# The last 64 rows of a Q projection in two row tiles, two heads at once, beside the paired remainder scores

## The chip, the cores and the metric

The kernel runs on one core of a Trainium2 chip. The metric is device time in microseconds of that core; lower is better. Engines are called PE (TensorE, the matrix unit), DVE (VectorE), ACT (ScalarE), POOL (GpSimd) and SP (SyncE, which here only issues DMAs). PE reads weights and a moving operand from SBUF and writes PSUM, which has eight banks; DVE and ACT read PSUM and write SBUF.

## The reference

Two independent problems A and B of the same shape are computed and their outputs are put side by side. Each is grouped-query attention against a cache of keys and values:

```python
B, Sq, D = 16, 80, 576
Hq, Hkv, Sk, Dh = 32, 16, 512, 128          # two query heads share one K/V head
q = (x @ wq)                                # [B*Sq, 576] @ [576, 4096]
scores = einsum("bhqd,bhkd->bhqk", q, k) * Dh ** -0.5
p = softmax(scores, axis=-1)
o = einsum("bhqk,bhkd->bhqd", p, v)
out = o @ wo                                # [B*Sq, 4096] @ [4096, 576]
result = concatenate([out_A, out_B], axis=-1)
```

All inputs are bfloat16. The contraction of the Q projection has 576 rows, which is four times 128 and a rest of 64.

## The kernel before, in words

**Units.** The work of both problems is cut into 128 units; a unit is one batch with four K/V heads, that is eight query heads of 80 rows. Eight units with the same heads form an octet (variable `goct`, 16 of them), which is what the Q projection works by. For each unit PE computes scores in five tiles: the 160 query rows of one K/V head are 128 + 32, so each of the four heads gives one main tile (line 658, 128 rows by 512 keys), and the four rests of 32 rows are put into one remainder tile by four matmuls that stand side by side in column tiles of 32 (line 644, `tile_position=(0, 32 * g4)`). The remainder tiles of two units are issued together as a group (`em_qkr`, lines 640 to 655; `GRP` and `GR` give the group sizes 1, 1, 2, 2, ...).

**A tile's way.** DVE takes the row maximum (line 667), ACT the exponential with the row sum (671), DVE the reciprocal (677), POOL the normalisation (680), PE four transposes (686), DVE the copy back to SBUF (692, 694), and PE multiplies with V (731). ACT evicts that result (747), and PE's output projection (781) reads it. For 45 units the transposes of the remainder tile are made by a DMA instead (698).

**The Q projection** (line 540, `em_qp`). x is held transposed in `xT`, five chunks of 128 rows; since 576 is 4.5 chunks, the fifth chunk takes x's last 128 columns (line 463, and 485 for problem B), of which the first 64 have already been used, and the weights that meet them are zeros (`wqz`, line 395: rows 0 to 63 of the fifth chunk of `wq_sb`). For each octet and each of its eight heads there are two pieces, one of six batches (480 columns) and one of two (160 columns); each piece is five matmuls into one PSUM bank, and one eviction with the scale, by ACT (551) or DVE (552), whichever the planner finds free. In the first octet the narrow piece comes first.

**Order.** Every operation is put into a list with a due time (`key`), what it reads and writes, and an assumed duration; the planner (`_Sched.arrange`, lines 135 to 253) runs through the list with these durations, takes at each engine the most urgent operation that is ready, and gives out PSUM banks from the list of the operation's class (`BANKS`: S scores, T transposes, O attention output, M, M0, M1, ML projections). The result is a fixed order for each engine, with semaphore waits between them. Each engine runs its own list in that order. A bank is given out again when its last reader is done. `ahead` moves an operation forward in the choice without moving its due time.

**DMAs.** All loads but the first two of `wq` are issued by SP, in one list: K by a transposing DMA (612) into five buffers, V (616) into four, `wq` in an "a" part (514, 512 rows) and a "b" part (517, the last 64 rows), `wo` (580), x of problem A as rows (449), which PE transposes (464) at the start, and x of problem B by transposing DMAs (481, 485).

## Time and profile before

| | us |
|---|---|
| median of three runs | 781.97 (780.68 to 783.51) |
| the profiled execution | 780.9 |
| its span on the core | 779.2 |
| PE busy | 772.0 |
| DVE busy | 678.6 |
| ACT busy | 611.6 |
| POOL busy | 432.4 |
| Q projection matmuls (line 540), 480 columns / 160 columns | 149.7 / 64.2 |
| remainder scores (line 644) | 39.6 |

The profile is of one execution. A busy time is the time in which at least one instruction of the engine or group was running; the durations of matmuls overlap, because they are pipelined and their ends are modelled, so the distance between the starts of matmuls that follow each other tells what one costs. "Idle before" is the time for which the engine stood idle just before instructions of a group, with the engine and line that released most of it.

### The profile page before, as it was taken

Reading aid. Unit: us, or ns where it says so; the run is one execution under the profiler, and the core shown is the slowest. Engines: PE = TensorE matmul, PEld = TensorE weight load, DVE = VectorE, ACT = ScalarE, POOL = GpSimd, SP = SyncE. Lnnn points to the kernel's source line nnn. Section 1 sums busy time; section 2 is a strip of 40 time slices with the busy share of each in tenths; the row PEclk is TensorE's granted clock in tenths of the full one; section 3 lists DMA queues with packets and bytes.
Section 4 is the critical chain, followed back from the end, with each engine's and each line's share of the span. In section 5 each row is a group of like instructions: output and inputs, shape, how many; then the busy total and the mean of one; then the engine's idle time right before and its main releaser. Section 6 shows DMA issues by size and latency. Waiting matters only on the chain.

```text
span 779.2 us, 21256 instructions
## 1 busy us (share of the span) xinstructions
PE 772.0 (99%) x8078; PEld 567.5 (73%) x8078; DVE 678.6 (87%) x1558; ACT 611.6 (78%) x1736; POOL 432.4 (55%) x647
## 2 busy tenths in 40 slices
PE   9999999999999999999999999999999999999998
PEld 5576677777777777767777777777777777777786
DVE  4999988888888899888898899988888888989982
ACT  1878988888888888867787777978888887887860
POOL 1555755565655656555655655655655655664660
PEclk9999999999999999999999999999999999999999
DMA  9999999988899999999999999999999978999951
GB/s 249 226 259 240 249 222 247 203 188 197 205 200 213 204 237 247 251 213 227 211 229 214 177 214 244 258 218 237 221 230 202 200 177 196 257 220 210 187 134 32
DMA packets 386564, 166.44 MB, mean 214 GB/s; under 512 B 300576, under 2 KB 383008, under 8 KB 386464
## 3 DMA queue, kind: packets, MB, share of 16 engines
q1 hardware_dynamic: 385248, 163.91, 95.7%
q8 instruction: 65, 1.06, 0.6%
q10 hardware_dynamic: 1216, 1.18, 0.5%
q14 instruction: 35, 0.29, 0.1%
HBM read 87.46 MB, written 2.95 MB: 116 GB/s over the span
## 4 chain that ended last, share of the span: by engine, by line
PE 91%; DVE 7%; DMA 1%; ACT 0%; POOL 0%; issue 0%; SPq 0%
PE ps L540 20%; PE ps L781 20%; PE ps L731 17%; PE ps L686 15%; PE ps L658 13%; DVE negmax L667 4%; PE ps L644 4%; DVE pT L694 2%; DVE qT L552 1%; DMA kT<-in_A_k_cache_dram 1%; PE ps L409 0%; PE ps L464 0%; DVE pT L692 0%; ACT p_sb L671 0%; PE ps L424 0%; POOL p_sb L680 0%
## 5 line engine op out<-in xcount | busy, mean ns | idle before, releaser
L680 POOL TENSOR_SCALAR p_sb<-p_sb,rinv 128x512 bf16<-128x512 bf16 x640 | 430.0, 692 | 325.5 <-DVE rinv L677 325.1
L671 ACT ACTIVATE p_sb<-ps,negmax 128x512 bf16<-128x512 f32 x640 | 441.3, 693 | 84.0 <-DVE negmax L667 77.1
L667 DVE TENSOR_REDUCE negmax<-ps 128x1 f32<-128x512 f32 x640 | 427.8, 679 | 9.6 <-PE ps L658 5.1
L686 PE MATMUL ps<-ident,p_sb 128*128 128x128 bf16 x2380 | 229.7, 219 | 1.1 <-POOL p_sb L680 0.5
L694 DVE COPY pT<-ps 128x512 bf16<-128x512 bf16 x512 | 209.9, 413 | 16.4 <-PE ps L686 14.2
L731 PE MATMUL ps<-pT,v_sb 128*128 128x160 bf16 x2048 | 222.6, 233 | 0.1
L540 PE MATMUL ps<-xT,wq_sb 128*128 128x480 bf16 (+1 forms) x1280 | 213.2, 300 | 0.1
L731 PEld LDWEIGHTS ps<-pT,v_sb 128*128 128x128 bf16 x2048 | 158.4, 98 | 54.3 <-ACT oT L747 5.9
L686 PEld LDWEIGHTS ps<-ident,p_sb 128*128 128x128 bf16 x2380 | 168.7, 98 | 35.7 <-DVE pT L694 6.5
L658 PE MATMUL ps<-kT,qT 128*128 128x512 bf16 x512 | 189.0, 379 | 0.6 <-ACT p_sb L671 0.6
L781 PE MATMUL ps<-wo_sb,oT 128*128 128x288 bf16 x1280 | 171.5, 286 | 0.0
L540 PEld LDWEIGHTS ps<-xT,wq_sb 128*128 128x128 bf16 x1280 | 106.9, 98 | 61.4 <-ACT oT L747 2.6
L781 PEld LDWEIGHTS ps<-wo_sb,oT 128*128 128x128 bf16 x1280 | 122.8, 98 | 34.8 <-ACT qT L551 1.3
L747 ACT CAST oT<-ps 128x320 bf16<-128x320 f32 x256 | 108.7, 425 | 37.0 <-PE ps L731 36.6
L671 ACT ACTIVATION_READ_ACCUMULATOR p_sb<-ps,negmax 128x1 f32 x640 | 130.1, 203 | 0.0
L551 ACT ACTIVATE qT<-ps 128x160 bf16<-128x160 f32 (+1 forms) x159 | 63.2, 398 | 25.9 <-PE ps L540 24.9
L552 DVE TENSOR_SCALAR qT<-ps 128x480 bf16<-128x480 f32 (+1 forms) x97 | 54.7, 564 | 22.2 <-PE ps L540 21.1
L658 PEld LDWEIGHTS ps<-kT,qT 128*128 128x128 bf16 x512 | 49.2, 98 | 6.3 <-ACT p_sb L671 3.1
L809 DVE TENSOR_TENSOR osb<-ps,acc 128x288 bf16<-128x288 f32 x40 | 18.2, 456 | 27.6 <-PE ps L781 27.4
L644 PE MATMUL ps<-kT,qT 128*32 128x512 bf16 x512 | 39.6, 384 | 1.1 <-DMA kT<-in_A_k_cache_dram 0.9
L677 DVE RECIPROCAL rinv<-rowsum 128x1 f32<-128x1 f32 (+1 forms) x173 | 29.6, 171 | 11.1 <-ACT p_sb L671 11.1
L692 DVE COPY pT<-ps 128x512 bf16<-128x512 bf16 x83 | 34.5, 416 | 4.9 <-PE ps L686 4.7
(19 smaller groups left out, 47.0 us busy)
## 6 DMA issues: line engine op xcount, KB each, us to landing
v_sb<-in_A_v_cache_dram SPq DMA_DIRECT2D x64, 512.0 KB, 4.6
v_sb<-in_B_v_cache_dram SPq DMA_DIRECT2D x64, 512.0 KB, 4.6
wo_sb<-in_A_wo_dram SPq DMA_DIRECT2D x8, 576.0 KB, 7.6
wo_sb<-in_B_wo_dram SPq DMA_DIRECT2D x8, 576.0 KB, 7.4
wq_sb<-in_B_wq_dram SPq DMA_DIRECT2D x4, 1024.0 KB, 6.7
out_dram<-osb SPq DMA_DIRECT2D x40, 72.0 KB, 2.3
wq_sb<-in_A_wq_dram SPq DMA_DIRECT2D x2, 1024.0 KB, 7.4
wq_sb<-in_A_wq_dram ACTq DMA_DIRECT2D x2, 512.0 KB, 6.9
```

Source lines behind the costliest of these rows:

```text
L540: last = e.matmul(ps[:, vb.phys, 0:n1 - n0], lhsT=wq_sb[:, wsl, ck, i * 128:(i + 1) * 128], rhs=xT[:, half, ck, n0:n1], start=(ck == 0), s ...
L551: return e.activation(dst, src, AF.Identity, scale=SCALE)
L644: last = e.matmul(ps[32 * g4:32 * g4 + 32, vb_.phys, :], lhsT=qT[:, qsl_, bl_, g4 * 160 + 128:g4 * 160 + 160], rhs=kT[:, ks_, :, g4 * 128: ...
L658: return e.matmul(ps[:, vb.phys, :], lhsT=qT[:, qsl, bl, gl * 160:gl * 160 + 128], rhs=kT[:, ks, :, gl * 128:(gl + 1) * 128], start=True, ...
L667: return e.tensor_reduce(negmax[:, si:si + 1], ps[:, vb.phys, :], axis=AX.X, op=AluOpType.max, negate=True)
L671: return e.activation(p_sb[:, psl, :], ps[:, vb.phys, :], AF.Exp, bias=negmax[:, si:si + 1], scale=1.0, accum_out=rowsum[:, ss, k:k + 1])
L680: return e.tensor_scalar(p_sb[:, psl, :], p_sb[:, psl, :], rinv[:, ss, k:k + 1], 1.0, op0=AluOpType.mult, op1=AluOpType.mult)
L686: last = e.transpose(psb[:, vt.phys, j * 128:(j + 1) * 128], p_sb[:, psl, j * 128:(j + 1) * 128], ident[:])
L694: return e.tensor_copy(pT[:, pts, :, 0:4, gl * 32:gl * 32 + 32], psb[:, vt.phys, 0:512].rearrange("p (j h c) -> p j h c", j=4, h=4))
L731: last = e.matmul(ps[:, vo.phys, off:off + 160], lhsT=v_sb[:, vs, gl, j * 128:(j + 1) * 128], rhs=pT[:, pts, j, :, gl * 32:gl * 32 + 32], ...
L747: return e.copy(dst, src)
L781: last = e.matmul(ps[:, vb.phys, 0:DC], lhsT=oT[:, hi, rb * 128:(rb + 1) * 128], rhs=wo_sb[:, wi, c3 * DC:(c3 + 1) * DC], start=(hi == 0), ...
```

## The change

The fifth matmul of the projection is taken apart. For the 480-column pieces it is no longer a full matmul with half of its rows zero. Instead, the last 64 rows of the weights of two neighbouring heads lie one above the other in a new tile `wq5` (head 2p in partitions 0 to 63, head 2p+1 in 64 to 127), the last 64 rows of x lie twice in chunk four of `xT` (both halves), and one matmul of 64 rows for each of the two heads is issued, at row tile positions (0, 0) and (64, 0), into a PSUM bank of its own (`em_q5`). These two start the accumulation; the four full matmuls of each head go on in the same bank. For octets 2 to 15 the pair is issued by the same operation as a group's remainder scores, right behind them (`attach`); for octets 0 and 1 it is an operation of its own. Both banks come from a new class Q = (6, 7, 4, 5), and are taken when the pair is issued.

The 160-column pieces keep five matmuls; the fifth takes the weights of both heads from `wq5` and as moving operand a tile `xz`, in which the other head's half is zero. They now hold batches 0 and 1, the wide pieces batches 2 to 7, in all octets.

To set up the data, x of problem A gets a copy of 64 columns before its transposes (`em_xdc`, DVE), x of problem B a DMA from one half of the chunk to the other (`em_xdup`), `xz` is cleared once and filled by two DVE copies for each half of each problem (`add_xz`), and each load of the last 64 rows of `wq` becomes two, with runs of one head (256 bytes). The zero rows of `wq_sb` go away.

The evictions of the attached wide pieces are given to ACT alone (`QEE`). Class M gets two more banks. Attention output evictions get `ahead` 8, those of the output projection 15. The due times of the projection, of x's second half (`XH`), and of the loads of `wq` and of x of problem B follow the groups now. `RSEL` selects the same 45 units as before.

```diff
+QOFF = 4
+QEE = (("act",), ("act",))
+QS = 4.0
+QD = 2.0
...
-BANKS = dict(S=(0, 1, 2, 6), T=(3, 4), O=(5, 7), M=(7, 5), M0=(7, 5, 6, 3, 4), M1=(7, 6), ML=(7, 5, 6, 0, 1))
+BANKS = dict(S=(0, 1, 2, 6), T=(3, 4), O=(5, 7), M=(7, 5, 6, 4), M0=(7, 5, 6, 3, 4), M1=(7, 6), ML=(7, 5, 6, 0, 1), Q=(6, 7, 4, 5))
...
-OEO = 0.0
-OVO = 0.0
+OEO = 8.0
+OVO = 15.0
...
-XH = -2.0
+XH = -12.0
...
-        wq_sb = sb("wq_sb", [128, 2, 5, 1024], BF16)
+        wq_sb = sb("wq_sb", [128, 2, 4, 1024], BF16)
+        wq5 = sb("wq5", [128, 2, 512], BF16)
+        xz = sb("xz", [128, 2, 2, 160], BF16)
...
-        def em_wqz(e):
-            return e.memset(wq_sb[0:64, :, 4, :], 0.0)
+        def em_xz(e):
+            return e.memset(xz[:], 0.0)
...
+        gkey = [Qof[(g_[0], 0)] - LA + 0.0 for g_ in groups]
+        attach = dict((i_, []) for i_ in range(len(groups)))
+        q5key = {}
+        for g_ in range(NG):
+            for p_ in range(4):
+                if g_ == 0:
+                    q5key[(g_, p_)] = (-LA - (3.6, 2.4, 0.5, -2.0)[p_], None)
+                elif g_ == 1:
+                    q5key[(g_, p_)] = (5.0 * (8 - QL2 + 2 * p_) + 1.6, None)
+                else:
+                    j_ = 4 * (g_ - 2) + p_
+                    j_ += 1 + int(QOFF * j_ / (4 * (NG - 2)))
+                    q5key[(g_, p_)] = (gkey[j_], j_)
...
+        def add_xz(prob, half, key, reads):
+            for par in range(2):
+                def em_xzc(e, half=half, par=par):
+                    return e.tensor_copy(xz[64 * par:64 * par + 64, half, par, :],
+                                         xT[64 * par:64 * par + 64, half, 4, 0:160])
+
+                S.add("dve", key + 0.001 * par, em_xzc, reads=reads,
+                      writes=[R(("xz", half), 1 + 2 * prob + par)], name="xzc%d.%d.%d" % (prob, half, par),
+                      stream="xev", dur=0.15, lat=0.13)
...
+                def em_xdc(e, half=half, k0=k0, k1=k1):
+                    rows = slice(half * NRT + k0, half * NRT + k1)
+                    return e.tensor_copy(xs[:, rows, D:D + 64], xs[:, rows, 512:D])
...
+            def em_xdup(e, half=half):
+                return e.dma_start(xT[0:64, half, 4, :], xT[64:128, half, 4, :])
...
+                def em_ldwb(e, wq_ap=wq_ap, q=q, wsl=wsl, c0=c0, c1=c1, par=0):
+                    src = wq_ap[512:576, q * 1024 + c0:q * 1024 + c1].rearrange("p (h w n) -> w p h n", w=2, n=128)
+                    return e.dma_start(wq5[64 * par:64 * par + 64, wsl, c0 // 2:c1 // 2], src[par])
...
-                        for ck in range(5):
+                        for ck in range(4):
                             last = e.matmul(ps[:, vb.phys, 0:n1 - n0],
                                             lhsT=wq_sb[:, wsl, ck, i * 128:(i + 1) * 128],
-                                            rhs=xT[:, half, ck, n0:n1], start=(ck == 0), stop=(ck == 4))
+                                            rhs=xT[:, half, ck, n0:n1], start=(c == 0 and ck == 0),
+                                            stop=(c == 1 and ck == 3))
+                        if c == 0:
+                            last = e.matmul(ps[:, vb.phys, 0:n1 - n0],
+                                            lhsT=wq5[:, wsl, (i // 2) * 128:(i // 2 + 1) * 128],
+                                            rhs=xz[:, half, i % 2, :], start=False, stop=True)
...
+                def em_q5(e, pr=pr, wsl=wsl, half=half, n0=n0, n1=n1, vbs=tuple(qres[(goct, pr)])):
+                    last = None
+                    for par in range(2):
+                        r0 = 64 * par
+                        last = e.matmul(ps[:, vbs[par].phys, 0:n1 - n0],
+                                        lhsT=wq5[r0:r0 + 64, wsl, pr * 128:(pr + 1) * 128],
+                                        rhs=xT[r0:r0 + 64, half, 4, n0:n1], start=True, stop=False,
+                                        tile_position=(r0, 0))
+                    return last
+
+                q5 = (em_q5, [R(("wq", wsl, "b%d" % p_, pr // 2), wv) for p_ in range(2)] + xr[1], qres[(goct, pr)],
+                      [R(("qT", qsl, bl, i_), goct) for bl in range(QB[1][0], 8) for i_ in (2 * pr, 2 * pr + 1)])
+                if gi is None:
+                    S.add("pe", kq, q5[0], reads=q5[1], writes=[R(v_, 0) for v_ in q5[2]] + q5[3],
+                          name="q5%d.%d" % (goct, pr), stream="Q", dur=_mm(1, n1 - n0) + 0.0105, lat=0.2,
+                          alloc=list(q5[2]), mode=2)
+                else:
+                    attach[gi].append(q5)
...
+                        q5s = attach[gof[U]]
+
+                        def em_qkr(e, group=tuple(group), q5s=tuple(q5s)):
...
+                            for f_ in q5s:
+                                last = f_[0](e)
...
+                              + [R(("kT", g_[2]), g_[0]) for g_ in group] + [r_ for q_ in q5s for r_ in q_[1]],
+                              writes=[R(g_[1], 0) for g_ in group] + [R(v_, 0) for q_ in q5s for v_ in q_[2]]
+                              + [r_ for q_ in q5s for r_ in q_[3]],
+                              name="qkr%d" % U, stream="S",
+                              dur=len(group) * (_mm(1, 512) + 0.0105) + len(q5s) * (_mm(1, 480) + 0.11), lat=0.2,
+                              alloc=[v_ for q_ in q5s for v_ in q_[2]] + [g_[1] for g_ in group], mode=2 if q5s else 1)
```

## The prediction

> **What bounds the kernel now.** I read the page's busy shares first, then the table by stage, then the groups with shapes kept apart, then the timeline of one stretch. Busy shares:
>
> ```profile
> span 779.2 us, 21256 instructions
> PE 772.0 (99%) x8078; PEld 567.5 (73%) x8078; DVE 678.6 (87%) x1558; ACT 611.6 (78%) x1736; POOL 432.4 (55%) x647
> PEclk9999999999999999999999999999999999999999
> ```
>
> TensorE has work for 772.0 of 779.2 us at the full granted clock. A busy matmul row can hide waiting (ends are modelled), so I look at pitches: the distance between starts. The table by stage (PE, PEld, DVE, ACT, POOL busy; clock; DMA share; GB/s):
>
> ```profile
> 20.00:60.00 40.00, 38.91 (x396) 26.17 (x395) 38.22 (x83) 31.31 (x92) 20.15 (x30) 1.00 1.09 244
> 100.00:300.00 200.00, 199.95 (x2124) 148.23 (x2122) 174.92 (x404) 170.19 (x486) 116.14 (x173) 1.00 0.99 212
> 320.00:340.00 20.00, 19.04 (x208) 14.06 (x206) 16.19 (x38) 13.59 (x40) 13.30 (x20) 1.00 1.02 241
> 340.00:500.00 160.00, 160.00 (x1679) 117.78 (x1677) 146.95 (x340) 127.26 (x358) 89.42 (x134) 1.00 1.02 221
> ```
>
> Between 100 and 300 us PE is idle for 0.05 us; only the ramp (20 to 60) and the change of problem (320 to 340) lose about 1 us each. One stretch of PE in order of time, start and length in us:
>
> ```profile
> 300.35 0.39 PE L686 MATMUL ps<-ident,p_sb 128*128 128x128 bf16 x4
> 300.67 0.62 PE L644 MATMUL ps<-kT,qT 128*32 128x512 bf16 x8
> 301.22 0.45 PE L731 MATMUL ps<-pT,v_sb 128*128 128x160 bf16 x4
> ...
> 302.35 0.39 PE L686 MATMUL ps<-ident,p_sb 128*128 128x128 bf16 x4
> 302.57 0.38 PE L658 MATMUL ps<-kT,qT 128*128 128x512 bf16 x1
> 302.79 0.39 PE L686 MATMUL ps<-ident,p_sb 128*128 128x128 bf16 x4
> 303.01 0.38 PE L658 MATMUL ps<-kT,qT 128*128 128x512 bf16 x1
> 303.23 1.18 PE L540 MATMUL ps<-xT,wq_sb 128*128 128x480 bf16 x5
> 304.24 0.44 PE L731 MATMUL ps<-pT,v_sb 128*128 128x160 bf16 x4
> ```
>
> Starts, not lengths, give the price. Five 480-column matmuls take 304.24-303.23 = 1.01 us, 0.202 each. Four transposes take 302.57-302.35 = 0.22. One 512-column matmul takes 302.79-302.57 = 0.22 (0.215 before rounding). Around the remainder scores (L644, four column tiles side by side, two sets) there are holes: the transposes at 300.35 leave PE free at 300.57, L644 starts at 300.67, so going into tiles costs 0.10; its two sets need 0.43 of the 0.55 until 301.22, so coming out costs about 0.11. Everything else abuts. So the bound is the sum of PE's columns plus these holes: a column taken from PE shortens the kernel unless a new wait or hole takes its place.
>
> **The change, part by part.**
>
> Removed: the fifth matmul of each of the 128 wide projection pieces.
>
> ```profile
> L540 PE MATMUL ps<-xT,wq_sb 128*128 128x480 bf16 x640 | 149.7, 366 | 0.1
> L540 PE MATMUL ps<-xT,wq_sb 128*128 128x160 bf16 x640 | 64.2, 233 | 0.0
> L644 PE MATMUL ps<-kT,qT 128*32 128x512 bf16 x512 | 39.6, 384 | 1.1 <-DMA kT<-in_A_k_cache_dram 0.9
> L552 DVE TENSOR_SCALAR qT<-ps 128x480 bf16<-128x480 f32 x71 | 46.5, 655 | 20.8 <-PE ps L540 19.9
> L551 ACT ACTIVATE qT<-ps 128x480 bf16<-128x480 f32 x57 | 32.4, 568 | 1.8 <-PE ps L540 1.3
> ```
>
> 640 = 128 x 5 become 128 x 4: 128 x 0.202 = 25.9 us off PE. The 160-column pieces keep five matmuls (the fifth reads the zeroed copy in place of xT): 0.
>
> Added: 64 pairs of 64-row matmuls of 480 columns. In the changed order 56 of them stand straight behind L644's eight, and 8 (octets 0 and 1) alone. No row tile is in this trace; the nearest row is L644's column tiles, whose four members run in the time of one (two sets in 0.43). If row tiles behave so, a pair streams 0.202 + 0.01; if they run one after the other, 0.404. I take the first, 0.21. Between column tiles and row tiles there may be a hole of 0 (both are tiled) up to 0.10 (as on entering); I take 0.10, the nearest row. The way out, 0.11, is paid today too. So an attached pair costs 0.31 (bounds 0.21 and 0.50) against 0.404 saved, and a lone pair 0.10 + 0.21 + 0.10 = 0.41, which is no gain. Sum: 56 x 0.31 + 8 x 0.41 = 17.4 + 3.3 = 20.7 us on PE. Net 25.9 - 20.7 = 5.2 us, with bounds of 10.8 (56 x 0.10 more) and -7.2 (64 x 0.194 less).
>
> The page "TensorEngine Tiling (Array Packing)" of the Trainium skill, Key Properties, says that a change of tiling mode, not merely of tile, drains TensorE; it speaks against a free step from column to row tiles, and by it alone the sum stays at 5.2. The page "TensorE: Matmul & The Clock Gate", Measured speedup vs the span model, lists 3.07x for four row tiles; an estimate from it at the same share for two tiles is 1.54x, 0.26 us a pair, and the sum would be 64 x 0.05 = 3.2 us worse, a gain of 2.0. L644 is here against that figure: its four members cost one matmul's pitch.
>
> Moved: evictions. In the changed order ACT takes 113 wide ones (57 before) and 75 narrow (102), DVE 15 wide (71) and 53 narrow (26). With 655 and 568 ns from the rows above, and narrow ones at 315 (DVE) and 304 ns (ACT), DVE loses 56 x 0.655 - 27 x 0.315 = 28.2 us and ACT gains 56 x 0.568 - 27 x 0.304 = 23.6. DVE goes to about 652 us and ACT to 635 of 774: 84% and 82%, neither the bound. 0 on the path.
>
> A lump: a group is now 0.10 + 0.43 + 0.31 + 8 x 0.202 = 2.5 us of PE without a new main score tile (behind 44 of the 64 pairs all eight wide matmuls follow at once). DVE gets two remainder tiles then, 2 x 0.679 (L667) = 1.4 us, so up to 1.1 us of DVE can run dry per two units (about 12 us, of which DVE has 16%, 1.9 us, spare). It fits, 0, with half of what it needs to spare; if cover is short, score tiles come late and PE waits at a transpose.
>
> Waits added: the remainder scores now also wait for two more PSUM banks (out of 6, 7, 4, 5, shared with scores, projection, transposes and PV) and the wq5 load. PE is in order, so behind them queue all transposes, PV and output matmuls. For 0: the bound from below. From above: the ramp shows single PE waits of 0.2 to 0.3 us for DVE and ACT. I take 0.01 per group, 0.6 us in all, since the order of before hides nearly all of such waits.
>
> DMA: eight-head loads of wq's last 64 rows become two with 256-byte runs; SP issues 8 and ACT 2 more such loads, and SP 2 SBUF copies, each issue about 0.6 us of a queue (ACT's four issues at the start last 0.49 to 0.65). At the start ACT's queue gets 1.2 us longer; the second half of wq would land near 12.6 instead of 11.4, first used near 14: hidden. Later loads stand 40 us or more of PE work ahead of their use. SP pushes K loads back by about 0.6 each time; by the trace's landing times K is there 10.9 us (median) before its first matmul. 0, or 1 us where problem B's loads meet (320 to 340 already loses 1.0).
>
> Start: four DVE column copies before the x transposes (between 59 ns, the small memset, and 484 ns, the xT copy), and eight small xz copies. x lands at 4.30 us and the first transpose runs at 4.63, behind the warm-up: 0 to 0.3 us; I take 0.1.
>
> The profiled execution: 780.9 - 5.2 + 0.6 + 0.1 = 776.4. The median of the runs shown, 781.97, stands 1.1 above it, so 777.5; I say 777.
>
> **Rivals.**
> - A, the forecast: side by side, one more hole per group, order still dense: 777 (775 to 779.5). Chance 0.52.
> - B, no hole between column and row tiles: 56 x 0.10 = 5.6 less, 771.5. For it: both are tiled. Against: every change of form in this trace costs 0.10. 0.10.
> - C, slower: the group waits for its two extra banks. The price decides at 5.2 / 56 = 0.09 us per group; a wait of 0.2 us, as the ramp shows, costs 56 x 0.2 = 11.2 and gives 788. For it: eight banks, and a group now wants four at once. Against: PE's idle time in the steady stages is 0.05 us in 200, and ACT and DVE have 16% or more to spare. 0.15.
> - D, slower: row tiles run one after the other, 64 x 0.19 = 12.3 more: 790. L644 speaks against it. 0.05.
> - E, half-way: waits or a longer weight load in the tiles take 0.04 to 0.08 us per group, 2 to 5 us: 779 to 782. 0.18.
>
> **How the numbers follow.** 0.3% is 2.3 us, what a measurement here can tell from no change: faster means under 779.6, slower over 784.3. Faster: A, B and 0.05 of E = 0.67. Slower: C and D = 0.20. The rest, 0.13, is the same. The range from 771 to 785 leaves out most of C, D and the best of B. A's own range is 775 to 779.5.
>
> **What would show it.** Right: PE still 99% busy; the row-tile matmuls start within 20 ns of each other; the wide piece behind them starts about 0.31 us after the last remainder set has streamed; the 480-column form at 512 instructions; PE's start-to-start holes elsewhere unchanged; DVE near 650 us and ACT near 635. Wrong: idle time in front of L727 released by ACT or DVE (C); the pair taking 0.40 us (D); no hole at the step (B); idle time at transposes after each lump, released by POOL (the lump); a late first score tile (the start).

## The result and the profile after

The changed kernel is slower by about 0.4%: 785.27 us (median of 20 runs, 780.90 to 789.25) against 781.22 us of the kernel before (20 runs, 779.75 to 783.51); the ratio is 1.0041, with a 95% interval of 1.0027 to 1.0055. The forecast was 777.0, in a range of 771 to 785. The sign is wrong, and the time lies just above the range.

The profiled execution of the changed kernel took 782.28 us, 3 us less than its median. Its page, in the lines that answer to those of before:

```profile
span 780.5 us, 21366 instructions
PE 768.9 (99%) x8078; PEld 558.0 (71%) x8078; DVE 658.1 (84%) x1541; ACT 626.2 (80%) x1765; POOL 433.5 (56%) x647
PEclk9999999999999999999999999999999999999999
```

TensorE's busy time is 3.1 us less than before (772.0), and the span is 1.3 us longer: its idle time went from 7.2 to 11.6 us. A busy time of matmuls hides part of the waiting, so the real split is worked out from starts below. The groups with shapes kept apart (busy us, mean ns, idle before) show that the work is what the forecast counted:

```profile
L606 PE MATMUL ps<-xT,wq_sb 128*128 128x480 bf16 x512 | 117.8, 367 | 0.0
L622 ACT ACTIVATE qT<-ps 128x480 bf16<-128x480 f32 x113 | 59.7, 569 | 2.4 <-PE ps L606 2.4
L727 PE MATMUL ps<-kT,qT 128*32 128x512 bf16 x512 | 39.6, 384 | 0.1
L647 PE MATMUL ps<-xT,wq 64*128 64x480 bf16 x128 | 24.1, 372 | 1.0 <-DVE xT L514 0.9
L623 DVE TENSOR_SCALAR qT<-ps 128x480 bf16<-128x480 f32 x15 | 9.8, 656 | 4.7 <-PE ps L606 4.3
```

The timeline of PE around one group with a pair (start and length in us):

```profile
308.26 0.39 PE L774 MATMUL ps<-ident,p_sb 128*128 128x128 bf16 x4
308.58 0.61 PE L727 MATMUL ps<-kT,qT 128*32 128x512 bf16 x8
309.13 0.38 PE L647 MATMUL ps<-xT,wq 64*128 64x480 bf16 x2
309.44 1.79 PE L606 MATMUL ps<-xT,wq_sb 128*128 128x480 bf16 x8
```

From the pair to the wide pieces it is 309.44-309.13 = 0.31 us: two matmuls of 480 columns stream in the time of one (they start 3 ns apart), and then comes a hole of 0.10. Between the column tiles (L727, 0.43 us of streaming from 308.58) and the row tiles there is a hole of 0.11. Over all 56 attached pairs the hole on the way in has a median of 96 ns, and that on the way out 102 ns (62 pairs).

So where did the time go? I went through PE's matmuls in order of their starts. A start is a wait where it comes more than 0.12 us later than the one before it plus that one's streaming (0.202 us for 480 columns, 0.216 for 512, 0.069 for 160, all pitches of this trace) and, at a change between full matmuls and tiles, a hole of 0.096 us. From 4.5 us on, summed by stage (us):

| profiled run | span | waits | span less waits | 4.5-30 | 30-100 | 100-300 | 300-345 | 345-490 | 490-520 | 520-720 | 720-end |
|---|---|---|---|---|---|---|---|---|---|---|---|
| before | 779.2 | 6.0 | 773.2 | 2.0 | 2.1 | 0.2 | 1.2 | 0 | 0 | 0.5 | 0 |
| after | 780.5 | 13.2 | 767.3 | 3.0 | 2.8 | 1.9 | 0.7 | 0 | 1.2 | 0.8 | 2.7 |
| again | 781.6 | 14.0 | 767.6 | 2.5 | 2.7 | 1.9 | 1.6 | 0.5 | 1.8 | 0.8 | 2.3 |
| again2 | 784.3 | 16.9 | 767.4 | 2.8 | 2.7 | 2.0 | 5.9 | 0 | 0.2 | 1.0 | 2.3 |
| start_order | 789.0 | 19.0 | 770.0 | 1.5 | 2.7 | 1.9 | 4.3 | 0.6 | 4.3 | 1.0 | 2.8 |
| wo_small | 775.0 | 7.8 | 767.2 | 1.3 | 2.7 | 1.9 | 0.7 | 0 | 0.4 | 0.8 | 0 |
| dlat26 | 778.1 | 10.5 | 767.6 | 1.3 | 2.7 | 1.9 | 1.8 | 0.6 | 1.0 | 1.0 | 0.2 |
| d26_b1 | 795.8 | 26.9 | 768.9 | 1.8 | 3.4 | 7.1 | 2.1 | 4.5 | 0.8 | 3.9 | 3.4 |
| q5_twice | 790.7 | 11.8 | 778.9 | 2.8 | 2.7 | 1.7 | 0.9 | 0 | 0.2 | 1.0 | 2.6 |
| no_q5 | 765.3 | 15.3 | 750.0 | 3.4 | 2.7 | 2.6 | 1.7 | 0.2 | 0.8 | 2.7 | 1.3 |

This table carries most of what follows. The work on PE fell by 773.2-767.3 = 5.9 us; the forecast had 5.2. The waits rose by 13.2-6.0 = 7.2 us; the forecast had 0.7. And the waits differ between executions of one and the same kernel: 13.2, 14.0 and 16.9 in three profiles, with the rest equal within 0.3 us.

The same in the profile's own words: stages of before, then of after (PE, PEld, DVE, ACT, POOL busy; clock; DMA share; GB/s).

```profile
0.00:20.00 20.00, 18.57 (x131) 10.50 (x132) 10.00 (x23) 3.99 (x9) 2.43 (x7) 1.00 0.99 246
500.00:520.00 20.00, 20.00 (x222) 15.30 (x221) 18.39 (x43) 16.67 (x50) 12.02 (x18) 1.00 1.08 222
720.00:748.00 28.00, 28.00 (x318) 21.95 (x317) 27.50 (x68) 23.74 (x66) 19.47 (x29) 1.00 0.99 212
```

```profile
0.00:20.00 20.00, 17.11 (x129) 9.46 (x130) 9.28 (x28) 2.80 (x6) 1.26 (x7) 1.00 1.04 242
100.00:300.00 200.00, 199.14 (x2120) 145.14 (x2119) 172.86 (x405) 171.22 (x488) 121.05 (x180) 1.00 1.00 210
500.00:520.00 20.00, 19.33 (x199) 13.74 (x197) 15.75 (x39) 17.16 (x50) 11.53 (x18) 1.00 0.94 235
720.00:748.00 28.00, 26.23 (x288) 19.17 (x286) 25.36 (x62) 22.71 (x63) 16.96 (x26) 1.00 0.96 221
```

Three things wait, each on another resource; the runs below add a fourth.

**The start.** DVE now copies 64 columns of x (L495) as each part of x lands, and DVE works in order. In its timeline the copy of a later part stands in front of evictions that are ready (the bracket is the idle time before, and what ended it):

```profile
8.62 0.20 DVE L495 COPY acc<-acc 128x128 bf16<-128x128 bf16 x1 [1.16 <-DMA acc<-in_A_x_dram]
8.74 0.49 DVE L514 COPY xT<-ps 128x640 bf16<-128x640 bf16 x1
...
10.87 0.23 DVE L495 COPY acc<-acc 128x192 bf16<-128x192 bf16 x1 [1.25 <-DMA acc<-in_A_x_dram]
11.01 0.47 DVE L514 COPY xT<-ps 128x640 bf16<-128x640 bf16 x1
```

and PE waits behind them, in its own timeline (L418 is a small memset on DVE that frees the warm-up's bank; it stands behind the same copy):

```profile
8.90 0.45 PE L509 MATMUL ps<-ident,acc 128*128 128x128 bf16 x5 [0.65 <-DVE wo_sb L418]
...
11.63 0.38 PE L647 MATMUL ps<-xT,wq 64*128 64x480 bf16 x2 [0.90 <-DVE xT L514]
```

**A PSUM bank on loan.** PE waits at PV matmuls five times for about 0.5 us (at 68.7, 91.1, 159.5, 260.9 and 307.1), 2.6 us in all, and at transposes four times for about 0.2 us (203.8, 215.2, 285.0 and 296.5), together 3.4 us. Six of the nine lie between 100 and 300 us, where before had 0.2 us of waits. One of the five at PV, and the ACT instruction that ends it:

```profile
259.82 0.44 PE L606 MATMUL ps<-xT,wq_sb 128*128 128x160 bf16 x4
260.10 0.23 PE L611 MATMUL ps<-xz,wq 128*128 128x160 bf16 x1
260.17 0.39 PE L774 MATMUL ps<-ident,p_sb 128*128 128x128 bf16 x4
260.87 0.45 PE L819 MATMUL ps<-pT,v_sb 128*128 128x160 bf16 x4 [0.31 <-ACT oT L835]
```

```profile
260.39 0.42 ACT L835 CAST oT<-ps 128x320 bf16<-128x320 f32 x1
```

By the planned order the narrow piece at 259.82 holds bank 7. The attention output has banks 5 and 7; PV therefore waits until the eviction from bank 5 is done at 260.39 + 0.42 = 260.81. At the other four PV waits, too, the planned order has a narrow piece in the second output bank. In before the projection could take banks 5 and 7 as well (class M), so the loan isn't new; that the two meet in these places is. The four waits at transposes are not a loan: by the planned order bank 4 holds the transposes just before, and bank 3 is still being copied out by DVE.

**A load that comes just too late.** The weights of the output projection (`wo`) are loaded anew for each of four sets, between the last use by one set and the first use by the next, and SP issues all loads in one list. SP's timeline in after, and then the last line's counterpart in before:

```profile
483.64 5.10 SPq L693 DMA_TRANSPOSE kT<-in_B_k_cache_dram  x1
488.78 0.58 SPq L903 DMA_DIRECT2D out_dram<-osb  x1
489.41 0.43 SPq L697 DMA_DIRECT2D v_sb<-in_B_v_cache_dram  x1
489.88 2.68 SPq L674 DMA_DIRECT2D wo_sb<-in_B_wo_dram  x4
```

```profile
485.93 2.93 SPq L580 DMA_DIRECT2D wo_sb<-in_B_wo_dram  x4
```

The four loads land at 500.90 in after and 496.12 in before; the first output matmul starts at 501.04 and 499.57. The slack, from the last landing to the first use, was 4.63, 3.45 and 8.92 us in before (sets two to four); in after it is 2.60, 0.14 and 2.34, in again 2.23, 0.14 and 3.05, in again2 0.14, 1.55 and 3.33, in start_order 0.14, 0.14 and 2.86. 0.14 us means that PE stood waiting for the load:

```profile
499.99 0.38 PE L746 MATMUL ps<-kT,qT 128*128 128x512 bf16 x1
501.04 0.77 PE L869 MATMUL ps<-wo_sb,oT 128*128 128x288 bf16 x5 [0.67 <-ACT p_sb L759]
```

The profile puts this one down to ACT, the landing at 500.90 says that it was the load. When loads land differs from execution to execution, and a slack of 2 us is eaten in some; between the profiled executions of after and again2 that makes most of the difference, and it probably makes the spread of 781 to 789 as well. SP's load isn't new: SP is busy issuing for 662 of the first 730 us in before and for 654 in after, and the DMA engines' share is 0.94 to 1.08 in the rows of both kernels above. The runs don't tell whether a late load waited for its turn in SP's list or for the engines.

At the end of the output stage (730 to 745 us) a fourth place loses 2.7 us, where before lost none; the runs below take it up.

### The profile page after: what moved, and what is told of

It is laid out like the page before. It is cut to its first block, busy times and chain, and to the rows that moved or that the text cites. A ratio compares the mean times of both kernels' runs of the same rounds, so it can differ in the third digit from the quotient of the medians.

```text
span 780.5 us, 21366 instructions
## 1 busy us (share of the span) xinstructions
PE 768.9 (99%) x8078; PEld 558.0 (71%) x8078; DVE 658.1 (84%) x1541; ACT 626.2 (80%) x1765; POOL 433.5 (56%) x647
## 3 DMA queue, kind: packets, MB, share of 16 engines
q8 instruction: 66, 1.08, 0.6%
## 4 chain that ended last, share of the span: by engine, by line
PE 86%; DVE 7%; ACT 4%; DMA 2%; issue 0%; SPq 0%; POOL 0%; DVEq 0%
PE ps L869 19%; PE ps L606 17%; PE ps L819 16%; PE ps L774 15%; PE ps L746 11%; PE ps L727 4%; DVE negmax L755 4%; ACT p_sb L759 3%; PE ps L647 3%; DVE pT L782 2%; DMA out_dram<-osb 1%; DMA acc<-in_A_x_dram 1%; PE ps L611 1%; ACT oT L835 1%; ACT qT L622 1%
## 5 line engine op out<-in xcount | busy, mean ns | idle before, releaser
L774 PE MATMUL ps<-ident,p_sb 128*128 128x128 bf16 x2380 | 224.1, 219 | 1.9 <-POOL p_sb L768 0.9
L774 PEld LDWEIGHTS ps<-ident,p_sb 128*128 128x128 bf16 x2380 | 164.7, 98 | 36.5 <-DVE pT L782 8.0
L746 PE MATMUL ps<-kT,qT 128*128 128x512 bf16 x512 | 185.5, 379 | 0.2 <-ACT p_sb L759 0.2
L869 PE MATMUL ps<-wo_sb,oT 128*128 128x288 bf16 x1280 | 180.1, 286 | 1.2 <-ACT p_sb L759 0.7
L606 PE MATMUL ps<-xT,wq_sb 128*128 128x480 bf16 (+1 forms) x1024 | 173.2, 300 | 0.2
L759 ACT ACTIVATION_READ_ACCUMULATOR p_sb<-ps,negmax 128x1 f32 x640 | 132.6, 207 | 0.0
L606 PEld LDWEIGHTS ps<-xT,wq_sb 128*128 128x128 bf16 x1024 | 83.6, 98 | 56.0 <-issue 13.4
L622 ACT ACTIVATE qT<-ps 128x480 bf16<-128x480 f32 (+1 forms) x188 | 82.6, 466 | 16.2 <-PE ps L611 13.4
L727 PE MATMUL ps<-kT,qT 128*32 128x512 bf16 x512 | 39.6, 384 | 0.1
L623 DVE TENSOR_SCALAR qT<-ps 128x160 bf16<-128x160 f32 (+1 forms) x68 | 26.3, 390 | 6.2 <-PE ps L606 4.3
```

The source lines that it names most:

```text
L606: last = e.matmul(ps[:, vb.phys, 0:n1 - n0], lhsT=wq_sb[:, wsl, ck, i * 128:(i + 1) * 128], rhs=xT[:, half, ck, n0:n1], start=(c == 0 and ...
L622: return e.activation(dst, src, AF.Identity, scale=SCALE)
L727: last = e.matmul(ps[32 * g4:32 * g4 + 32, vb_.phys, :], lhsT=qT[:, qsl_, bl_, g4 * 160 + 128:g4 * 160 + 160], rhs=kT[:, ks_, :, g4 * 128: ...
L746: return e.matmul(ps[:, vb.phys, :], lhsT=qT[:, qsl, bl, gl * 160:gl * 160 + 128], rhs=kT[:, ks, :, gl * 128:(gl + 1) * 128], start=True, ...
L759: return e.activation(p_sb[:, psl, :], ps[:, vb.phys, :], AF.Exp, bias=negmax[:, si:si + 1], scale=1.0, accum_out=rowsum[:, ss, k:k + 1])
L774: last = e.transpose(psb[:, vt.phys, j * 128:(j + 1) * 128], p_sb[:, psl, j * 128:(j + 1) * 128], ident[:])
```

## The experiments

They set the price of the work on PE apart from the waits, and try to set the four waits apart from each other. Ratios are against the kernel before on the same chip; before's own median was 781.85 (again to prio0 in the table), 779.83 (q5_twice to dlat26), 781.56 (again2 to before_d26) and 780.15 us (the rest), so medians from different chips are not compared directly.

| run | median us | ratio | 95% interval |
|---|---|---|---|
| again | 786.27 | 1.0050 | 1.0026 to 1.0074 |
| start_order | 783.58 | 1.0025 | 1.0002 to 1.0048 |
| osb3 | 785.41 | 1.0042 | 1.0025 to 1.0060 |
| prio0 | 786.66 | 1.0062 | 1.0040 to 1.0083 |
| q5_twice | 790.91 | 1.0143 | 1.0129 to 1.0157 |
| no_q5 | 767.45 | 0.9842 | 0.9827 to 0.9857 |
| wo_small | 777.30 | 0.9964 | 0.9951 to 0.9976 |
| dlat26 | 780.54 | 1.0013 | 1.0004 to 1.0021 |
| again2 | 786.22 | 1.0068 | 1.0044 to 1.0092 |
| d26_b1 | 795.19 | 1.0185 | 1.0168 to 1.0201 |
| d26_o3 | 782.10 | 1.0014 | 1.0001 to 1.0026 |
| before_d26 | 780.89 | 0.9988 | 0.9977 to 0.9998 |
| d26_q | 785.32 | 1.0065 | 1.0053 to 1.0077 |
| d26_m | 789.36 | 1.0120 | 1.0107 to 1.0133 |
| opx | 782.26 | 1.0028 | 1.0017 to 1.0040 |
| d32 | 783.34 | 1.0033 | 1.0020 to 1.0046 |

### again, again2: the changed kernel once more

> The changed kernel once more, for a second profile and to compare the others with. Theory: PE's columns and holes come out as forecast (5.2 us net off PE), and about 7 us of new PE waits (start 2, output stage 2.7, the rest in between) and a few more in most executions give it back: 785, slower than before by 0.4%. The holes and columns of this profile are the same as in the first; the waits differ from execution to execution, most of all where DVE waits for a store. Rival: the extra 3 us of the median execution lie in the holes between tile forms, and are the same in kind everywhere.

> The changed kernel a third time, beside the next three on one chip. Theory: 782 to 786, again over the kernel before, with the waits at the start (about 2 us), at PV for the attention output's bank (five of 0.5 us) and in the output stage in the same places, and the wait for wo near 500 us varying between executions. Rival (the slowness belonged to the chips of the earlier runs): level with the kernel before or faster.

The kernel is unchanged, so there is no diff. Both are again slower than before (1.0050 and 1.0068). Their profiles have the same work on PE (767.6 and 767.4) and other waits. From after to again2 the span grows by 3.8 us and the waits by 3.7; 5.9 us of again2's waits stand between 300 and 345 us, where the second set of `wo` came late (2.77 us at 316.6) and a V load at 336.0 (1.81 us).

### q5_twice, no_q5: is the price of the pair right?

```diff
+                                last = f_[0](e, stop=True)
                                 last = f_[0](e)
```

> The 56 attached pairs are issued twice, straight after one another; every other instruction stands where it stood. Theory (a pair streams in the time of one matmul, and PE's columns set the time): 56 x 0.21 = 11.8 us more than the changed kernel, and the trace shows the second pair 0.2 us after the first, with no hole. Rival 1 (row tiles one after the other): 23 us more. Rival 2 (PE waits so often that columns are free): 0 to 5 us more.

```diff
-                            for f_ in q5s:
-                                last = f_[0](e)
```

> The 56 attached pairs are left out, with the step from column to row tiles; the wide pieces of octets 2 to 15 lack the last 64 rows of the contraction, every other instruction stands where it stood. Theory (PE's columns set the time): 56 x 0.31 = 17.4 us less than the changed kernel, less what turns into new waits, so 768 to 773. Rival (other engines' order or the DMAs have become the bound): no more than 8 us less.

q5_twice issues each of the 56 attached pairs twice. no_q5 leaves them out: the last 64 rows of the contraction are missing from 56 of the 64 wide pairs. In both the planner's assumed durations were left alone, so the order stays that of after.

Span less waits: 778.9-767.3 = 11.6 us for the second pair, 11.6 / 56 = 0.207 us each; 767.3-750.0 = 17.3 us for the pair left out, 17.3 / 56 = 0.309 each. The forecast had 0.21 for a pair and 0.31 with its hole. PE's timeline in q5_twice around one doubled pair, 0.51 us to the wide pieces in place of 0.31:

```profile
313.18 0.62 PE L727 MATMUL ps<-kT,qT 128*32 128x512 bf16 x8
313.73 0.58 PE L647 MATMUL ps<-xT,wq 64*128 64x480 bf16 x4
314.24 1.79 PE L606 MATMUL ps<-xT,wq_sb 128*128 128x480 bf16 x8
```

That settles the price of the pair: the loss isn't in it. The medians (1.0143 and 0.9842) follow the work only in part. Against 1.0041 to 1.0068 of the changed kernel, no_q5 gains 16 to 18 us, as its work says, and ends just under its expected 768 to 773; q5_twice loses 6 to 8 us where 11.8 were expected. The longer work on PE leaves the loads more time: the slack of the three `wo` sets is 3.87, 1.58 and 4.00 us in q5_twice and 0.20, 0.14 and 1.95 in no_q5, against 2.60, 0.14 and 2.34 in after.

### start_order: the copies of x behind the evictions

```diff
-                S.add("dve", XLD[half][part] + 0.3, em_xdc,
-                      reads=[R(("xs", half * NRT + k_), 0) for k_ in range(k0, k1)],
+                S.add("dve", (XA + 6.5 if half else XA + 1.2) if part or half else XLD[half][part] + 0.3, em_xdc,
+                      reads=[R(("xs", half * NRT + k_), 0) for k_ in range(k0, k1)]
+                      + ([R(("xT", 0, 4), 0)] if half else [R(("xT", 0, 1), 0)] if part else []),
```

> DVE's copies of x's last 64 columns (three of the four) are put behind the evictions of the x transposes that stood behind them; PE's, POOL's and SP's orders are the same instruction for instruction. Theory (DVE waits in order for x's DMA, and with it the evictions that PE needs): PE's waits at 8.9 and 11.6 us go (0.8 and 1.0 us), time 1.5 to 2 us less than the changed kernel. Rival (PE would wait for x or wq itself there): 0.

The orders of PE, POOL and SP stay; DVE's changes, and one eviction goes from DVE to ACT. The median is 2.7 us below that of again on the same chip, though the intervals of the two ratios overlap. In the profile the waits at 8.9 and 11.6 us are gone, and the waits up to 30 us fall from 3.0 (after) to 1.5 us, below before's 2.0. The first pair (L647 in after) starts at 11.63, 11.27 and 11.15 us in after, again and again2, and at 10.50, 9.65 and 9.72 in start_order, wo_small and dlat26, which have this edit. So the copies cost about 1.4 us, not the 0.1 of the forecast.

This run's profile is also the worst case of the late load. PE's timeline:

```profile
503.04 0.38 PE L747 MATMUL ps<-kT,qT 128*128 128x512 bf16 x1
506.68 2.08 PE L870 MATMUL ps<-wo_sb,oT 128*128 128x288 bf16 x8 [3.26 <-DMA wo_sb<-in_B_wo_dram]
508.55 0.63 PE L747 MATMUL ps<-kT,qT 128*128 128x512 bf16 x1
```

Eight output matmuls take 508.55-506.68 = 1.87 us, where eight cost 0.98 elsewhere, and in the table by stage the granted clock (third number from the end) is one half from the middle of the wait on:

```profile
503.30:505.50 2.20, 0.12 (x1) 0.00 (x0) 1.72 (x5) 2.00 (x6) 0.69 (x1) 1.00 1.64 202
505.60:506.60 1.00, 0.00 (x0) 0.00 (x0) 0.00 (x0) 0.00 (x0) 0.00 (x0) 0.50 0.35 81
507.00:509.00 2.00, 2.00 (x10) 1.11 (x9) 0.00 (x0) 0.00 (x0) 0.00 (x0) 0.50 0.79 171
509.00:512.00 3.00, 3.00 (x19) 2.19 (x18) 2.50 (x6) 1.77 (x5) 0.18 (x1) 0.50 0.94 236
```

So this wait costs more than its 3.4 us: span less waits is 2.7 us higher than in after, and the starts between 506.7 and 512.4 us, where the clock rises again, make up for all of it. The page "TensorE: Matmul & The Clock Gate" of the Trainium skill, Part 1 (the HAM clock gate), says that the clock is set by how busy the array was in an activity window of about 3.4 us. The size fits, but the window itself isn't shown: here the clock fell about 2.3 us after the last matmul had streamed, and after the 2.61 us of idle time before 316.57 in again2 it was still at full.

### osb3, prio0: the end of the output stage

```diff
-NOSB = 2
+NOSB = 3
```

> Three output slots in place of two; nearly the same order on every engine. Theory (in the output stage DVE, with its urgent output addition in front, waits for a store of two additions ago, and row maxima behind it come late): idle time of DVE before the output addition, released by the store's DMA, goes, PE's waits of 2.7 us between 730 and 745 us go, time 2 to 5 us less than the changed kernel, and less spread. Rival (these waits are PSUM waits that happen to lie there): 0 to 0.5 us less, DVE idle before the additions unchanged.

```diff
-OEO = 8.0
-OVO = 15.0
+OEO = 0.0
+OVO = 0.0
```

> Attention output and output projection evictions lose the lead of 8 and 15 (OEO = OVO = 0, as in the kernel before); the rest as changed. Theory (the lead of the output addition puts DVE in front of unfinished stores): the tail's waits go as with three slots, 2 to 4 us less than the changed kernel; PE may wait more for ACT at PV. Rival (the lead is what keeps PE from waiting for PSUM): slower than the changed kernel by 2 us or more.

In after, DVE's output additions wait for a store two additions ago; its timeline:

```profile
735.74 0.46 DVE L897 TENSOR_TENSOR osb<-ps,acc 128x288 bf16<-128x288 f32 x1 [0.81 <-DMA out_dram<-osb]
743.88 0.46 DVE L897 TENSOR_TENSOR osb<-ps,acc 128x288 bf16<-128x288 f32 x1 [0.47 <-DMA out_dram<-osb]
```

With a third buffer those waits for a store are gone, and PE waits nevertheless, 2.5 us instead of 2.7 after 720 us:

```profile
732.74 0.44 PE L819 MATMUL ps<-pT,v_sb 128*128 128x160 bf16 x4 [0.72 <-ACT p_sb L759]
743.95 0.44 PE L819 MATMUL ps<-pT,v_sb 128*128 128x160 bf16 x4 [1.48 <-issue]
```

The remainder tiles that these PV matmuls read are transposed by a DMA that SP issues between K loads; the two landed at 732.65 and 743.86. The time is 0.9 us below again, within the noise, where 2 to 5 were expected. The theory that the stores alone cause this loss has fallen: behind the store stands another transfer of the same queue. Going back to the old priorities, expected to gain 2 to 4 us, doesn't help either (1.0062 against 1.0050), so the priorities are not the cause.

### wo_small, dlat26, before_d26, d26_o3, d32, opx: the queue of loads

```diff
+                        if ci >= NWC:
+                            return e.dma_start(wo_sb[:, wos * hc:wos * hc + 1, 0:32],
+                                               src.rearrange("(h p) n -> p h n", p=128)[:, 0:1, 0:32])
```

> On top of start_order, the twelve wo loads after the first four move 32 columns of one head in place of 576 columns of four (later output projections multiply with old weights); PE, DVE, ACT and POOL stand as in start_order. Theory (wo's third load lands when PE already waits, 0.8 to 3.4 us, and the loads push V and the remainder tile's DMA back): PE's waits near 314 and 501 to 507 us go, time 2 to 4 us under start_order's and less spread. Rival (the spread comes from elsewhere): same time and spread as start_order.

wo_small is start_order with the last twelve `wo` loads cut to 32 columns of one head, so the output projections of the last three sets use old weights. The order of all engines is kept. The time is 777.30, 0.9964 of before: faster, by 0.6% against start_order's 1.0025, and with a spread of 0.6 us over five runs. The slack of the three sets is 7.86, 5.77 and 7.45 us. The stages of its profile:

```profile
500.00:520.00 20.00, 20.00 (x205) 14.00 (x203) 15.21 (x35) 16.92 (x51) 12.74 (x19) 1.00 1.07 237
520.00:720.00 200.00, 199.86 (x2132) 147.79 (x2132) 172.62 (x408) 171.15 (x484) 116.49 (x174) 1.00 0.91 198
720.00:748.00 28.00, 28.00 (x317) 21.70 (x315) 27.88 (x68) 24.82 (x69) 18.02 (x27) 1.00 0.83 210
```

With 7 MB less in the queue the wait at 500 us is gone, and also all 2.7 us after 720 us, where no `wo` load is near: in after SP is busy issuing for 654 of the first 730 us, here for 598, and the small DMAs between the K loads come in time. So late DMAs cost after about 0.8 + 2.7 us in its profiled execution, and more in the median one. It isn't shown how much of the gain is the wait itself and how much the lighter traffic, and the kernel before wasn't run with the lighter loads; in its profile only 0.5 us of waits stand after 345 us.

dlat26 is start_order with the planner told that every load lands 1 us later; d32 tells it 1.6 us. before_d26 is the kernel before with dlat26's edit, as a control; d26_o3 adds osb3's buffer to dlat26; opx shifts when the output projections of sets two and three are due, and their loads with them, since both due times hang on the same number.

```diff
-DLAT = 1.6
+DLAT = 2.6
```

> On top of start_order, the planner counts one more microsecond for every DMA to land (DLAT 2.6 for 1.6), so that what waits for a load is put later in PE's order; the computation is whole. Theory (loads land later than the plan thinks): PE's waits for wo, V and the remainder tile's DMA shrink, 1 to 4 us under start_order, which would be level with the kernel before or better. Rival (the plan only shifts its waits): within 1 us of start_order.

> Control: the kernel before, with the same microsecond more for every DMA in the plan (DLAT 2.6). Theory (the kernel before has few waits for DMAs to lose): within 1.5 us of the kernel before, so what dlat26 gains belongs to the changed kernel's order. Rival (any order of this program gains from it): 2 us or more under the kernel before.

> On top of dlat26, three output slots. Theory (with loads planned later the stores no longer hold DVE): within 1 us of dlat26. Rival (stores still hold DVE in the output stage): 1.5 us or more under it.

> DLAT 3.2 in place of dlat26's 2.6. Theory (the plan is then later than the loads in nearly all executions): as dlat26 or up to 2 us less, level with the kernel before or under it. Rival (every plan has its own waits, and dlat26 drew a good one): 1 us or more above dlat26.

```diff
-OPX = ((12.0, 1.8), (18.5, 1.45), (18.5, 1.45), (18.5, 1.45))
+OPX = ((12.0, 1.8), (19.2, 1.4), (19.2, 1.4), (18.5, 1.45))
```

> On top of start_order, the output projections of A's second and B's first half are due 0.7 units (4 us) later, and 3% closer together; the plan counts DMAs as in the changed kernel. Theory (wo's load is late by 0.8 to 3.4 us at its first use): PE's waits for wo near 314 and 501 us go, 1 to 3 us less than start_order and less spread. Rival (the waits move to other places): as start_order.

In dlat26's profiled execution, the fastest of its eleven, the slack is 3.54, 3.62 and 3.48 us; its median is 1.0013 of before. It is built on start_order (1.0025), so its own gain is 0.12%, within start_order's interval and no more than the control's: the same parameter makes before itself 0.12% faster. Its expected gain of 1 to 4 us over start_order isn't shown. What does change is the spread, 2.7 us over eleven runs against 10.8 over start_order's twelve. d26_o3, with the same parameter, comes to 1.0014 on the chip where after stood at 1.0068, so a third output buffer adds nothing; in its profiled execution, one of its slowest, two sets again have a slack of 0.14 us. More of the same (d32, 1.0033) and a later output stage (opx, 1.0028) are not better: each makes another order, with waits elsewhere (d32 has 2.5 us between 345 and 490 us, where after has none), and in opx the third set's slack is 0.14 us as before. So dlat26 may just have drawn a good order, as the rival of d32 said. The best complete versions of the changed kernel stand within 0.15% of before, and none beats it.

### d26_q, d26_m, d26_b1: giving bank 5 back

```diff
-BANKS = dict(S=(0, 1, 2, 6), T=(3, 4), O=(5, 7), M=(7, 5, 6, 4), M0=(7, 5, 6, 3, 4), M1=(7, 6), ML=(7, 5, 6, 0, 1), Q=(6, 7, 4, 5))
+BANKS = dict(S=(0, 1, 2, 6), T=(3, 4), O=(5, 7), M=(7, 6, 4), M0=(7, 5, 6, 3, 4), M1=(7, 6), ML=(7, 5, 6, 0, 1), Q=(6, 7, 4))
```

The diff is that of d26_b1, on top of dlat26: bank 5 is taken from the pairs' class Q and from the projection's class M. d26_q takes it from Q alone, d26_m from M alone.

> On top of dlat26, the pair's two banks come from (6, 7, 4) only; the narrow pieces and output projections may still take bank 5. Theory (two banks for a pair, at the same moment as two for the remainder scores, are what the eight banks are short of): waits in front of the remainder scores and behind them, released by DVE and ACT, 5 to 14 us more than dlat26. Rival (bank 5 is not needed by the pair): within 1.5 us of dlat26.

> On top of dlat26, narrow pieces and output projections take (7, 6, 4) and no longer bank 5; the pair may. Theory (the five waits of 0.5 us at PV come from a narrow piece in the other output bank): they go, and the time is 0 to 2.5 us less than dlat26. Rival (those pieces need the bank; the loss of 14 us in d26_b1 was theirs): 5 us or more above dlat26.

> On top of dlat26, bank 5 belongs to the attention output alone: M = (7, 6, 4), Q = (6, 7, 4). Theory (the five waits of 0.5 us at PV, released by ACT's eviction of the same bank, are there because a narrow projection piece holds the other output bank): these waits go, 2 to 3 us less than dlat26. Rival (the plan needs the lent banks; their lack shows as waits at the projection or at the remainder scores): as much or more than dlat26.

If the loan of bank 5 were simply a mistake, giving it back would end the PV waits. Instead the ratios are 1.0065, 1.0120 and 1.0185 against dlat26's 1.0013: slower by 4, 8 and 13 us. The PV waits go down from five to two in d26_q and three in d26_b1, but stay at five in d26_m; bank 7 is still lent in all three. The groups of waits between 100 and 300 us (total us, times, longest), the row of transposes waiting for DVE's copy in dlat26 and then in d26_b1:

```profile
PEld ps L775 <- DVE pT L783: 1.5, 7, 0.3
```

```profile
PEld ps L775 <- DVE pT L783: 6.9, 23, 0.7
```

In d26_q and d26_b1 the waits move to the transposes and multiply. Each of the three is also a new order, and the loss stands in its plan: run through the durations that the planner assumes, the lists end at 786.0, 790.9 and 795.0 us, against 781.8 for dlat26, which is 4, 9 and 13 us later. So the eight banks are short, in the plan as on the chip: one bank withheld from the pairs and the projection costs far more than its loan costs the output. The page "TensorEngine Tiling (Array Packing)" of the Trainium skill, Gotcha 1 (PSUM Pressure), says that different row tiles write to different PSUM banks and so raise the pressure on PSUM. These runs agree; with one of its four banks withheld from the pairs' class alone, this kernel lost 4 us of 780.

## Why the prediction was wrong

**What held.** Removed columns, the pair at 0.21 and its hole at 0.10, the lone pairs without gain: the sum of 5.2 us less on PE measured 5.9. The two runs on the pair give 0.207 and 0.309 us. DVE came to 658 us (forecast 652) and ACT to 626 (635), neither the bound. Rival B (no hole) and D (one after the other) are out: the hole is 96 ns, the pair takes one matmul's time. The estimate of 0.26 us per pair, from the speedup for four row tiles in the page "TensorE: Matmul & The Clock Gate" (Measured speedup vs the span model), was too dear: the measured 0.207 decides.

**Two slips.** Rival D's 64 x 0.19 is 12.2, not 12.3, and gives 789. "The wide piece behind them starts about 0.31 us after the last remainder set has streamed": in after it is 309.44 - (308.58 + 0.43) = 0.43 us, since the way out of the tiles comes on top of the 0.31, as the sum itself had it ("is paid today too").

**The step that failed** is "I take 0.01 per group, 0.6 us in all, since the order of before hides nearly all of such waits"; with the 0.1 for the start and the 0 for the DMAs it makes 0.7 us. The waits rose by 7.2 us in the profiled execution of after (by stage: 1.0 up to 30 us, 1.9 from 30 to 345, 1.5 from 490 to 720, 2.7 behind), and by 10.9 in that of again2, which lies near the median. The 0.05 us of idle time in 200 us was read as a property of the work, that DVE and ACT with 16% to spare hide whatever comes. It was a property of one particular order, which had few microseconds of slack on three resources, and the change makes another order.

Part of the rise stood in the plan already. Run through the durations that the planner assumes, the list of before ends at 779.6 us and that of after at 777.6: the planned gain was 2.0 us, not 5.2, with 3.1 us more idle time on PE (2.9 against 1.0 between 100 and 300 us). The other 4.1 us of after came only in execution, most of it at the start, at the third set of `wo` and at the end.

Rival C named the resource (banks) but put the wait in the wrong place. L727 has 0.1 us of idle time before it in after; the 1.1 us before the same matmuls in before were nearly all for a K load. The group itself hardly waits; PV matmuls do, whose second bank holds a narrow piece. C's price "from which it decides", 5.2 us in all, was exceeded by several causes together, of which the five PV waits make 2.6 us.

**"Start: 0 to 0.3 us; I take 0.1."** The argument looked at PE's first transpose. Missing was what is queued behind the waiting instruction on DVE: the copies of x's later parts wait up to 1.25 us for their DMA in front of evictions. The runs put it at about 1.4 us.

**"DMA: 0, or 1 us where B's loads meet."** The number used, K landing 10.9 us ahead of its use, still holds (11.7 in after), but it is a median, and a median says nothing of the latest load. In the very profile that the forecast read, one K load landed only as PE stood waiting for it (338.7 us, the loss that the forecast names), and the third set of `wo` had 3.45 us; one K load in front of it holds SP for 5.1 us in after (3.7 in the median). The term is 0.8 us for `wo` and 2.7 us at the end in the profiled execution of after. In that of start_order, the slowest of its twelve, late loads cost 3.6 us around the second set and 3.4 at the third, with a drop of the clock. This is probably also why the median stands 3 us above the profiled execution, where the forecast added 1.1.

**What stays open.** Whether a better order exists that keeps the 5.9 us. wo_small shows the forecast gain to about half with part of the loads left out; no complete version here got below before. It also stays open which of SP's list and the busy DMA engines makes the loads late, and the 2.7 us at the end are traced to late transfers only by wo_small, where they vanish with the lighter loads.

## What to carry to other kernels

Where an engine is 99% busy under a planned order, the columns that a change saves can be counted exactly, but the absence of waits can't be carried over to the new order: for each resource that the change touches, look up the smallest slacks in the old trace (last landing to first use, last eviction to next use of a bank), not the median, and compare them with one more instruction of that queue. If a planner makes the order, its own planned end is a forecast too, and here it was nearer (2.0 us of gain). Split a result into span less waits, and waits by stage; it tells in one step whether the price or the order was wrong. Where executions of a kernel spread more than before, look for a load whose slack is about the spread.

## What the runs showed of the hardware

A change between column tiles and row tiles costs TensorE as much as one between tiles and full matmuls: 96 ns in, 102 ns out. Two 64-row tiles stream in the time of one matmul: 0.207 us for 480 columns, measured by doubling. In an idle time of 3.26 us on TensorE the granted clock fell to one half, about 2.3 us in, and stayed there for the first 5.7 us of work, which cost 2.7 us more; an idle time of 2.61 us left it at full. A transposing K load held SP for 3.7 us in the median, a V load for 0.6.
